# First loads in a new order, smaller and larger buffers, and another pacing of the inverse's tail

## The chip, the core and the metric

The kernel runs on one core of a Trainium2 chip. The time is device microseconds of one execution. A core has five engines that work in order, each with its own queue of instructions: TensorE (PE) multiplies, VectorE (DVE) and ScalarE (ACT) work element by element, GpSimd (POOL) does a few small operations here and casts while it transfers, SyncE (SP) only issues transfers. SP, ACT and POOL each issue DMA transfers from their own queue. SBUF holds the working tiles (128 partitions), PSUM the results of matmuls.

## What is computed

Four layers on x of 2048 x 576 in float32: two kinds, each used twice. A is a Fourier mixing of the normalized input; B is a gate by a long convolution that doesn't depend on x, so its value is the same in both uses.

```python
x = A_x
x = x + _A_ref(_layernorm(x), dft_seq_re, dft_seq_im, dft_hid_re, dft_hid_im)
x = x + _B_ref(_layernorm(x), B_k, B_v, B_shift_k, B_ssm_k, B_ssm_D)
x = x + _A_ref(_layernorm(x), ...)          # the same matrices
x = x + _B_ref(_layernorm(x), ...)          # the same k, v and kernels
...
# _A_ref:  y = Cr @ (x Wr^T) - Ci @ (x Wi^T)
# _B_ref:  kv = shift_conv(k, 4 taps) * v
#          y = causal_long_conv(kv, ssm_k) + kv * ssm_D ;  return q * y
```

## The kernel before

**Precision.** All matmuls are float32 to a reduced format (float32r). Each factor is split into a high part (ACT copies it, which rounds: line 84) and a low part (DVE subtracts: line 85), and a product is three matmuls: high by high, high by low, low by high. `split` is used for the C matrices, x, the weights and the convolution's data, so most rows of the profile bear these two lines.

**Layer A.** It takes U = C x first, then U W. `layer` walks four blocks of 512 columns (`tb`), two matrices (`g`, real and imaginary) and 16 row tiles (`k`): 128 steps n of 14 matmuls of 128 x 512 into PSUM tiles `s0` to `s3` and `rm`. For each step a C tile of 256 KB is loaded into a raw tile (`load_c`, ring `craw`, three tiles of NT = 512 words) and split into one of three tiles of the ring `cs`. The loads of step n + 2 are issued at step n, behind the previous C load (`load_after`: not before the last C load in the issue order, the `anchor`). A block's columns are multiplied by W later in `hidden`, in pieces of 27 matmuls of 128 x 288, which `finish` puts between the steps. `done0` stores the result xa.

**Branch B** is a generator, `branch`, whose steps are put between those of layer one. The long convolution is a transform of length 4096, factored in three parts. *F1* (steps n to 40): for 16 values of j and two sources (ssm_k and the gated k, v) a constant f1c is loaded (POOL, cast on the way), the source is built on DVE and split, twelve matmuls are made and four evacuations by ACT (line 395) fill two store buffers `so`, which ACT's queue stores to DRAM (`t`, line 396). Then W is loaded (`load_w`, raw ring `wl` of five) at steps 41 to 43. *Middle* (64 groups): load from `t` into a landing tile `land`, split to `df`, six matmuls with the constant `mc` (from midc), the spectra's product on DVE and ACT through `kk`, `p2` and `yf`, and, two groups later, three matmuls of the inverse, an evacuation by ACT into `vo` (line 449) and a store to `vd`. *Inverse, or i2* (32 pieces): the constant i2c is loaded by POOL into `fc`, a row of `vd` by SP into `land`, split, and six matmuls, evacuated into `vo` (line 460) and stored to `yb`. Twelve pieces run between the last middle groups, 20 behind them.

**Pacing.** Between step 44 (`W_END` + 1) and 111 (`I2_END`) the generator yields a number for each piece of its work, 3.1 for a middle group in all, 1.2 for an i2 piece, and is resumed until the sum spent has reached that share of the whole (`work`) which the steps' planned time has reached.

**Between the layers.** From step 113 (`PREP`) on, `get_x1` builds layer two's x: it loads xa, reads yb, gates (`gated`, DVE), stores xb, normalizes, stores y and splits the result into `mats`. Layer two does its first block in the same way and the other three by a Strassen scheme of seven products (`strassen`), which the change touches only by the C ring's size in the first 14 steps.

**Memory.** `flts` is one flat tile, whose words from `SC_AT` on hold the raw C tiles, and behind them, in turn, F1's buffers (`so`, `v`, `tmp`), the raw weights (`wl`), the middle's buffers (`res`, `kk`, `land`, `vo`, `p2`) and xa and yb. A tile laid over the words of an older one waits for its last use.

**The instruction order** on each engine's queue is fixed when the kernel is built, by a scheduler that follows the program's order and its own plan of times; it may put an instruction ahead of others of the same engine. In the built program of before, the start on PE is 24 f1 products, then the first step of layer one; SP's first issues are ssm_k, x, C, ssm_k, ssm_d, x, C.

Of the kernel before, what the change touches and what calls it, by code (L numbers as in the profile page):

```python
# [12 lines left out]
AF = mybir.ActivationFunctionType  # L13
# [9 lines left out]
NC = 4  # L23
REM = D - NC * P
EPS = 1e-5
PRE = 2
ASTAT = 8
XLEAD = 3
K_FIRST = 2
# [6 lines left out]
MID_LAG = 2  # L36
I2_FIRST = 37
I2_LATE = 4
PIECE = 3.6
STEP = 3.2  # L40
KP = 4
H = 2 * P
WIDE = 2 * NT
KR = 5
STAT = 20
STATIC = 14
B_LOAD = 15
# [10 lines left out]
def fnet_h3_kernel(ctx: ExitStack, tc: tile.TileContext, x, c_mat, w_re, w_im, k_pad, v, shift_k,  # L58
# [38 lines left out]
    def region_b(dt, name):  # L97
        return sb.tile([P, 6 * WIDE], dt, tag="rb", name=name)
# [11 lines left out]
    def lay(t, at, *sizes):  # L110

        for name, words, n in sizes:
            ring.setdefault(name, Ring()).tiles.extend(t[:, at + i * words:at + (i + 1) * words] for i in range(n))
            at += n * words
        assert at <= t.shape[1], (at, t.shape, sizes)
        return at

    def fresh(*names):
        for name in names:
            ring[name] = Ring()  # L120
# [24 lines left out]
            return nc.sync.dma_start(dst, src).ins  # L145

    def load_fr(dst, src):
        if pows:
            with tc.issue_after(pows[-1]):
                nc.gpsimd.dma_start(dst, src)  # L150
        else:
            nc.gpsimd.dma_start(dst, src)

    nc.vector.memset(mhalf, -0.5)
# [47 lines left out]
    W = []  # L202

    def load_w():
        lay(flts, SC_AT + 3 * NT, ("wl", D, 5))
        wg = region_a(FR, "w").rearrange("p (k n) -> p k n", k=9)
        for ch in range(9):
            w = two(wg[:, ch])
            raw = ring["wl"]()
            if ch < 8:  # L210
                nc.sync.dma_start(raw, (w_re if ch < 4 else w_im)[(ch % 4) * P:(ch % 4 + 1) * P, :])
            else:
                nc.sync.dma_start(raw[:REM], w_re[NC * P:, :])
                nc.sync.dma_start(raw[REM:], w_im[NC * P:, :])
            for lo, hi, sg in ((0, P, 1 if ch < 4 else -1),) if ch < 8 else ((0, REM, 1), (REM, P, -1)):
                if sg > 0:
                    split(w[lo:hi, 0, :], w[lo:hi, 1, :], raw[lo:hi])
                else:
                    nc.scalar.activation(w[lo:hi, 0, :], raw[lo:hi], AF.Copy, scale=-1.0)
                    nc.vector.scalar_tensor_tensor(w[lo:hi, 1, :], raw[lo:hi], -1.0,  # L220
                                                   w[lo:hi, 0, :].bitcast(F32), op0=OP.mult,
                                                   op1=OP.subtract)
            W.append(w)
            yield
        for ch in range(9):
            load_after(w_d[ch], wg[:, ch].bitcast(F32))
            yield
# [95 lines left out]
    def quads(v):  # L323
        return v.rearrange("p (a q) -> p a q", a=4)

    def branch():
        wt = []
        f1r = region_b(FR, "f1r")
        lay(f1r, 0, ("xf", 2 * D, 4), ("fc", 4 * P, 3))
        lay(flts, SC_AT + 3 * NT, ("so", D, 3), ("v", D, 2), ("tmp", D, 1))  # L330
        f1f = region_a(F32, "f1f")
        lay(f1f, 0, ("k", 2 * D, KR), ("wt", 2 * D, 2), ("land", D, 3), ("v", D, 1))

# [19 lines left out]
        def f1_loads(j, src):  # L353
            if j not in fcs:
                fcs[j] = quads(ring["fc"]())
                load_fr(fcs[j], f1c[j])
            r = ring["land" if src else "v"]()
            nc.sync.dma_start(r, (ssm_k if src else v)[:, j, :])
            if not src:
                if not wt:  # L360
                    load_w4()
                while loaded[0] < min((J + 4) // 2, 2 + j, j // 2 + KR):
                    load_k(loaded[0])
                    loaded[0] += 1
            return r, fcs[j]
# [42 lines left out]
        f1_products(*xf)  # L408
        yield
        m1 = region_b(FR, "mid")  # L410
        at = lay(m1, 0, ("df", 2 * D, 3), ("mc", 4 * P, 1))
        fresh("land", "fc")
        spare = at
        at = lay(m1, at, ("yf", D, 2))
        lay(m1, at, ("fc", 4 * P, 2))
        lay(flts, SC_AT + 3 * NT, ("res", D, 2), ("kk", D, 2), ("land", D, 2), ("vo", HD, 2), ("p2", HD, 1))
        mc = quads(ring["mc"]())
        raw = ring["kk"]()[:, :4 * P]
        nc.sync.dma_start(raw, midc.rearrange("p a q -> p (a q)"))
        nc.scalar.activation(mc, quads(raw), AF.Copy)  # L420
        lo, hi = slice(0, 64), slice(64, 128)

        def mid_forward(df):
# [72 lines left out]
        for i, (kind, hf, q) in enumerate(feeds):  # L496
            df, fc = halves.pop(i)
            if kind:
                i2_products(hf, q, fc, df)
            else:  # L500
                if len(yfs) == MID_LAG:
                    mid_inverse(*yfs.pop(0))
                    yield 0.4
                yfs.append((hf, q, mid_forward(df)))
            split_feed(i + 1)
            load_feed(i + 2)
            if i == last_mid:
                while yfs:
                    yield 0.4
                    mid_inverse(*yfs.pop(0))  # L510
                old = ring["fc"]
                held = [old.tiles[(old.n + m) % 2] for m in range(2)]
                fresh("fc")
                lay(m1, spare, ("fc", 4 * P, 2))
                ring["fc"].tiles.extend(held)
            yield 1.2 if kind else 2.7

    def gated(xa, j, late=False):
        mv, rs, _ = norm_stats(xa)
        q = ring["yb"]()  # L520
        (load_after if late else nc.sync.dma_start)(q, yb_d[j])
        nc.vector.scalar_tensor_tensor(q, xa, mv[:, 0:1], q, op0=OP.subtract, op1=OP.mult)
        nc.vector.scalar_tensor_tensor(q, q, rs, xa, op0=OP.mult, op1=OP.add)
        return q
# [15 lines left out]
    def load_x(j):  # L540
        if j < J:
            XL[j] = ring["x"]()
            nc.sync.dma_start(XL[j], x[:, j, :])
# [12 lines left out]
    def get_x1(j):  # L556
        if j in ready:
            return
        ready.add(j)
        xa = ring["xa"]()  # L560
        nc.sync.dma_start(xa, xa_d[j])
        xb = gated(xa, j)
        nc.sync.dma_start(xb_d[j], xb)
        y = normed_x(xb, xa, ring["xj"]())
        stored.append(nc.sync.dma_start(y_d[j // 2][:, j % 2, :], y).ins)
        X[j] = to_x(y, j)
# [2 lines left out]
        nc.sync.dma_start(out[:, j, :], gated(xa, j, True))  # L569

    pending = []
    lay(flts, SC_AT, ("craw", NT, 3))
    br = branch()
    wl = load_w()
    for used in range(1, K_FIRST + 1):
        next(br)
        load_x(used - 1)
        if used <= 2:
            load_c((0, 0, used - 1))
        if used == PRE:  # L580
            get_x0(0)
        if used == PRE + 1:
            get_x0(1)
    spent, total, paced = 0.0, 0.0, [0.0]

    def pieces(n):
# [4 lines left out]
    for n in range(W_END + 1, I2_END + 1):  # L591
        total += STEP + PIECE * pieces(n)
        paced.append(total)
    work = 64 * 3.1 + 32 * 1.2
    for n, whole in layer(get_x0, lambda j: x[:, j, :], done0, pending):
        if whole and n <= F1_END:
            want = K_FIRST + (F1_16 * n // 16 if n <= 16 else F1_16 + (32 - K_FIRST - F1_16) * (n - 16) // (F1_END - 16))
            while used < want:
                next(br)
                used += 1  # L600
            if n == F1_END:
                next(br)
        if whole and F1_END < n <= W_END:
            for _ in range(3):
                next(wl, 0)
        if n > W_END:
            if whole and pieces(n):
                finish(pending, 1)
            m = n - W_END - 1
            if m + 1 < len(paced):  # L610
                done_by = paced[m] + (paced[m + 1] - paced[m] if whole else STEP * 3 / 7)
            else:
                done_by = total
            while spent < work * done_by / total:
                spent += next(br, work)
        if not whole:
            continue
        if n >= W_SAVE and n % 2 == 0:
            next(wl, 0)
        m = n - PREP  # L620
        if m == 0:
            lay(flts, SC_AT + 3 * NT + 2 * D, ("xa", D, 2), ("yb", D, 2))
            lay(region_b(F32, "gate"), 0, ("xa", D, 4), ("yb", D, 4), ("xj", D, 2))
        if 0 <= m < TB * (TB - 1):
            get_x1(m)
# [318 lines left out]
```

## Time and profile before

| | us |
|---|---|
| median of the three runs shown (1243.41 to 1248.4) | 1248.28 |
| the profiled execution | 1246.32 |
| its span, first to last instruction | 1244.5 |

The stages in the profiled execution: F1 to about 208, the weights to 226, middle groups to about 600, the i2 tail to 652, building of layer two's x to about 706, layer two's first block to 845, the Strassen products to 1123, the last hidden products to the end.

A busy time is the time in which an engine executes; the idle time before an instruction is named with what ended it (`[1.67 <-ACT flts L395]`: PE sat idle for 1.67 us until ACT's instruction of line 395 was done). Tiles are named by the flat tile that holds them: `flts` is most buffers, `mid` and `f1r` the branch's matmul factors, `mats` x and the split C, `bk`, `s` and `rm` PSUM tiles, `early` the input x.

### The profile page before, as it was taken

Reading aid. Unit: us, or ns where it says so; the run is one execution under the profiler, and the core shown is the slowest. Engines: PE = TensorE matmul, PEld = TensorE weight load, DVE = VectorE, ACT = ScalarE, POOL = GpSimd, SP = SyncE. Lnnn points to the kernel's source line nnn. Section 1 sums busy time; section 2 is a strip of 40 time slices with the busy share of each in tenths; the row PEclk is TensorE's granted clock in tenths of the full one; section 3 lists DMA queues with packets and bytes.
Section 4 is the critical chain, followed back from the end, with each engine's and each line's share of the span. In section 5 each row is a group of like instructions: output and inputs, shape, how many; then the busy total and the mean of one; then the engine's idle time right before and its main releaser. Section 6 shows DMA issues by size and latency. Waiting matters only on the chain.

```text
span 1244.5 us, 18406 instructions
## 1 busy us (share of the span) xinstructions
PE 1192.8 (96%) x6320; PEld 1031.2 (83%) x6320; DVE 847.5 (68%) x1559; ACT 658.4 (53%) x1315; POOL 81.5 (7%) x116
## 2 busy tenths in 40 slices
PE   6999999899999999999789999999999999999997
PEld 5778888798888888888677798888878878879997
DVE  6999894668776676766338844666667668674674
ACT  6865565658766676765347823534344344460210
POOL 2210000000000000000213201000000000000111
PEclk9999999999999999999899999999999999999999
DMA  8989987646656665566788863765475478687631
GB/s 282 316 254 288 285 251 247 203 132 175 196 186 188 186 191 176 167 182 191 224 260 275 283 195 112 254 223 167 138 254 159 133 265 274 232 270 229 217 118 41
DMA packets 145968, 261.97 MB, mean 210 GB/s; under 512 B 15825, under 2 KB 44497, under 8 KB 145874
## 3 DMA queue, kind: packets, MB, share of 16 engines
q1 hardware_dynamic: 102674, 205.73, 52.6%
q10 hardware_dynamic: 36288, 42.48, 9.8%
q0 software_dynamic: 6912, 12.59, 3.9%
q8 instruction: 50, 0.82, 0.3%
q14 instruction: 44, 0.36, 0.1%
HBM read 194.09 MB, written 66.65 MB: 210 GB/s over the span
## 4 chain that ended last, share of the span: by engine, by line
PE 67%; DMA 14%; DVE 9%; ACT 6%; issue 3%; POOL 1%; SPq 0%; ACTq 0%; POOLq 0%; DVEq 0%
PE s L67 35%; PE bk L67 27%; PE rm L67 5%; DMA ph<-in_c_mat 2%; DMA flts<-in_c_mat 2%; DVE mats L85 1%; DMA flts<-vd 1%; DMA t<-flts 1%; ACT mats L84 1%; DMA vd<-flts 1%; DMA yb<-flts 1%; DVE ph L720 1%; DVE mid L85 1%; DMA gate<-xa 1%; ACT mid L84 1%
## 5 line engine op out<-in xcount | busy, mean ns | idle before, releaser
L67 PE MATMUL s<-mats 128*128 128x512 f32 x2094 | 527.1, 393 | 6.5 <-DVE mats L85 2.0
L67 PEld LDWEIGHTS s<-mats 128*128 128x128 f32 x2094 | 387.1, 189 | 84.6 <-DVE mats L85 6.0
L84 ACT ACTIVATE mats<-flts 128x512 fp32r<-128x512 f32 x209 | 130.6, 626 | 110.7 <-PE rm L67 66.7
L85 DVE TENSOR_TENSOR mats<-flts,mats 128x512 fp32r<-128x512 f32 x209 | 143.4, 688 | 59.3 <-ACT mats L84 56.2
L67 PE MATMUL bk<-mid 128*128 128x288 f32 x768 | 128.4, 303 | 16.8 <-ACT mid L84 4.9
L67 PEld LDWEIGHTS bk<-mid 128*128 128x128 f32 x768 | 113.5, 190 | 34.2 <-ACT mid L84 6.9
L85 DVE TENSOR_TENSOR mid<-flts,mid 128x576 fp32r<-128x576 f32 (+1 forms) x160 | 101.0, 637 | 53.2 <-ACT mid L84 50.2
L84 ACT ACTIVATE mid<-flts 128x576 fp32r<-128x576 f32 (+1 forms) x160 | 93.2, 586 | 64.8 <-DVE flts L438 38.2
L67 PE MATMUL bk<-w,u 128*128 128x288 f32 x864 | 119.7, 295 | 2.0 <-ACT flts L449 1.1
L67 PEld LDWEIGHTS bk<-w,u 128*128 128x128 f32 x864 | 117.4, 188 | 5.1 <-ACT flts L449 1.5
L67 PE MATMUL rm<-mats 128*128 128x512 f32 x338 | 104.8, 390 | 1.9 <-DVE flts L252 1.9
L67 PEld LDWEIGHTS rm<-mats 128*128 128x128 f32 x338 | 63.5, 188 | 15.4 <-issue 2.3
L67 PE MATMUL bk<-f1r 128*128 128x288 f32 x384 | 62.6, 307 | 11.8 <-DMA f1r<-in_f1c 6.0
L67 PEld LDWEIGHTS bk<-f1r 128*128 128x128 f32 x384 | 57.8, 196 | 17.8 <-ACT flts L395 7.0
L164 POOL TENSOR_TENSOR flts<-flts 128x1 f32<-128x1 f32 x40 | 35.4, 884 | 557.0 <-DVE flts L163 554.9
L67 PE MATMUL s<-t,mats 128*128 128x512 f32 x258 | 64.5, 389 | 0.0
L395 ACT ACTIVATE flts<-bk 128x288 f32<-128x288 f32 x128 | 48.1, 409 | 23.4 <-DMA t<-flts 12.6
L67 PEld LDWEIGHTS s<-t,mats 128*128 128x128 f32 x258 | 48.4, 188 | 10.1
L67 PE MATMUL bk<-mats 128*128 128x288 f32 (+1 forms) x340 | 56.7, 309 | 0.0
L435 DVE TENSOR_TENSOR flts<-bk,flts 128x288 f32<-128x288 f32 x64 | 29.2, 456 | 39.7 <-ACT flts L431 38.1
L67 PEld LDWEIGHTS bk<-mats 128*128 128x128 f32 x340 | 48.8, 188 | 2.0
L67 PE MATMUL s<-mats,u 128*128 128x512 f32 x198 | 50.0, 390 | 0.0
(148 smaller groups left out, 1530.0 us busy)
## 6 DMA issues: line engine op xcount, KB each, us to landing
flts<-in_c_mat SPq DMA_DIRECT2D x150, 256.0 KB, 3.5
ph<-in_c_mat SPq DMA_DIRECT2D x48, 512.0 KB, 4.1
t<-flts ACTq DMA_DIRECT2D x64, 288.0 KB, 4.1
flts<-t SPq DMA_DIRECT2D x64, 288.0 KB, 3.2
flts<-in_c_mat SPq DMA_DIRECT2D x36, 512.0 KB, 4.7
vd<-flts ACTq DMA_DIRECT2D x64, 144.0 KB, 3.2
flts<-vd SPq DMA_DIRECT2D x32, 288.0 KB, 3.5
mid<-in_i2c POOLq DMA_DIRECT2D x32, 256.0 KB, 4.9
```

The lines of the kernel that those rows point to most:

```text
L67: nc.tensor.matmul(ps, lhsT, rhs, start=first, stop=last, skip_group_check=more)
L84: nc.scalar.activation(h, src, AF.Copy)
L85: nc.vector.tensor_tensor(l, src, h.bitcast(F32), OP.subtract)
L164: pows.append(nc.gpsimd.tensor_tensor(rs, ve, mhalf, OP.pow).ins)
L395: nc.scalar.activation(so[:, c, :], ps[:, :HD], AF.Copy)
L435: nc.vector.tensor_tensor(p1, px[:, :HD], p1, OP.mult)
L720: nc.vector.tensor_tensor(src, src, r, OP.add)
```

## The change

- **First loads.** The loop that issued F1's first loads and x's first loads together is written out: x tile 0, then the branch's first step, C, x tile 1, C, normalization of x tile 0, the branch's second step. The first f1c is no longer cast by POOL but loaded by SP to a raw tile and copied by ACT; the later ones wait in POOL's order for the first power (`pows`). In the built program x tile 0 is SP's first issue, then f1c, ssm_k, C, x, C, x, ssm_k; on PE 12 f1 products stand ahead of the first step.
- **Two raw C tiles** instead of three (`CRAW`). The 512 words go to others: four `so` instead of three, seven `wl` instead of five, three `vo` instead of two.
- **midc** is loaded by POOL straight to `mc`, in place of an SP load into a `kk` tile and a copy by ACT.
- **The i2 tail.** After the last middle group `land` has four tiles: the two of `kk` are free and join. From there loads are issued four pieces ahead instead of two. An i2 piece counts 2.0 in the pacing instead of 1.2 (`I2_COST`).
- **Layer two's x:** the loads of xa and yb in `get_x1` go behind the last C load in the issue order.

```diff
+I2_COST = 2.0
+CRAW = 2
     def load_fr(dst, src):
-        if pows:
-            with tc.issue_after(pows[-1]):
-                nc.gpsimd.dma_start(dst, src)
-        else:
+        with tc.issue_after(pows[-1]):
             nc.gpsimd.dma_start(dst, src)
...
-        lay(flts, SC_AT + 3 * NT, ("wl", D, 5))
+        lay(flts, SC_AT + CRAW * NT, ("wl", D, 7))
...
-        lay(flts, SC_AT + 3 * NT, ("so", D, 3), ("v", D, 2), ("tmp", D, 1))
+        lay(flts, SC_AT + CRAW * NT, ("so", D, 4), ("v", D, 2), ("tmp", D, 1))
...
                 fcs[j] = quads(ring["fc"]())
-                load_fr(fcs[j], f1c[j])
+                if pows:
+                    load_fr(fcs[j], f1c[j])
+                else:
+                    raw = quads(ring["tmp"]()[:, :4 * P])
+                    nc.sync.dma_start(raw, f1c[j])
+                    nc.scalar.activation(fcs[j], raw, AF.Copy)
...
+        kk_at = SC_AT + CRAW * NT + 2 * D
...
-        lay(flts, SC_AT + 3 * NT, ("res", D, 2), ("kk", D, 2), ("land", D, 2), ("vo", HD, 2), ("p2", HD, 1))
+        at = lay(flts, SC_AT + CRAW * NT, ("res", D, 2))
+        lay(flts, at, ("kk", D, 2), ("land", D, 2), ("vo", HD, 3), ("p2", HD, 1))
         mc = quads(ring["mc"]())
-        raw = ring["kk"]()[:, :4 * P]
-        nc.sync.dma_start(raw, midc.rearrange("p a q -> p (a q)"))
-        nc.scalar.activation(mc, quads(raw), AF.Copy)
+        load_fr(mc, midc)
...
-            load_feed(i + 2)
+            load_feed(i + (4 if i > last_mid else 2))
             if i == last_mid:
                 while yfs:
                     yield 0.4
                     mid_inverse(*yfs.pop(0))
-                old = ring["fc"]
-                held = [old.tiles[(old.n + m) % 2] for m in range(2)]
-                fresh("fc")
-                lay(m1, spare, ("fc", 4 * P, 2))
-                ring["fc"].tiles.extend(held)
-            yield 1.2 if kind else 2.7
+                for name, t, at, words in (("fc", m1, spare, 4 * P), ("land", flts, kk_at, D)):
+                    old = ring[name]
+                    held = [old.tiles[(old.n + m) % 2] for m in range(2)]
+                    fresh(name)
+                    lay(t, at, (name, words, 2))
+                    ring[name].tiles.extend(held)
+                load_feed(i + 3)
+                load_feed(i + 4)
+            yield I2_COST if kind else 2.7
...
         xa = ring["xa"]()
-        nc.sync.dma_start(xa, xa_d[j])
-        xb = gated(xa, j)
+        load_after(xa, xa_d[j])
+        xb = gated(xa, j, True)
...
-    lay(flts, SC_AT, ("craw", NT, 3))
+    lay(flts, SC_AT, ("craw", NT, CRAW))
     br = branch()
     wl = load_w()
-    for used in range(1, K_FIRST + 1):
-        next(br)
-        load_x(used - 1)
-        if used <= 2:
-            load_c((0, 0, used - 1))
-        if used == PRE:
-            get_x0(0)
-        if used == PRE + 1:
-            get_x0(1)
+    load_x(0)
+    next(br)
+    load_c((0, 0, 0))
+    load_x(1)
+    load_c((0, 0, 1))
+    get_x0(0)
+    next(br)
+    used = K_FIRST
...
-    work = 64 * 3.1 + 32 * 1.2
+    work = 64 * 3.1 + 32 * I2_COST
```

More of the change, by code (lines that the diff above doesn't have):

```diff
@@ L25 @@
 EPS = 1e-5
-PRE = 2
 ASTAT = 8
@@ L621, in fnet_h3_kernel @@
         if m == 0:
-            lay(flts, SC_AT + 3 * NT + 2 * D, ("xa", D, 2), ("yb", D, 2))
+            lay(flts, SC_AT + CRAW * NT + 2 * D, ("xa", D, 2), ("yb", D, 2))
             lay(region_b(F32, "gate"), 0, ("xa", D, 4), ("yb", D, 4), ("xj", D, 2))
```

## The prediction

> **What bounds the kernel now.** I read the page first, then a table of stretches, then PE's waits, then the order of time around each wait that the diff touches.
>
> ```profile
> span 1244.5 us, 18406 instructions
> PE 1192.8 (96%) x6320; PEld 1031.2 (83%) x6320; DVE 847.5 (68%) x1559; ACT 658.4 (53%) x1315; POOL 81.5 (7%) x116
> ```
>
> PE is the bound: 51.7 us of its span is idle (1244.5 - 1192.8), and no other engine is near. The matmuls stay the same in number, so the change can win only idle time of PE and time at a lowered clock. The stretches show where that is (columns: PE, PEld, DVE, ACT, POOL busy, granted clock, DMA share, GB/s; the last two rows are from a second table of this view):
>
> ```profile
> 0.00:25.00 25.00, 15.65 (x56) 12.90 (x57) 15.94 (x52) 16.09 (x30) 5.17 (x12) 0.93 0.85 277
> 50.00:75.00 25.00, 24.09 (x111) 19.58 (x109) 24.05 (x50) 18.03 (x37) 6.30 (x7) 1.00 0.88 288
> 325.00:350.00 25.00, 23.06 (x114) 19.16 (x113) 18.50 (x34) 19.18 (x42) 0.00 (x0) 0.97 0.59 185
> 550.00:575.00 25.00, 25.00 (x149) 22.50 (x148) 15.68 (x31) 16.29 (x36) 1.06 (x2) 1.00 0.66 195
> 600.00:625.00 25.00, 18.87 (x95) 15.50 (x95) 6.82 (x12) 8.31 (x17) 3.77 (x7) 0.86 0.88 269
> 625.00:650.00 25.00, 20.90 (x131) 18.57 (x130) 8.94 (x14) 10.52 (x20) 3.69 (x7) 1.00 0.88 260
> ...
> 590.00:646.00 56.00, 44.85 (x251) 38.41 (x251) 19.95 (x36) 21.47 (x43) 10.71 (x20) 0.94 0.80 239
> 655.00:706.00 51.00, 48.02 (x204) 37.38 (x203) 44.51 (x127) 38.97 (x81) 16.64 (x20) 1.00 0.86 280
> ```
>
> The reader is to see two holes: the first 25 us (9.35 idle) and 590 to 646, the inverse's tail (11.15 idle, clock 0.94). In that tail DVE and ACT are idle for most of the time and the transfers are busy for 0.88: its limit is data that comes late.
>
> **The change part by part.**
>
> *First loads.* The order at the start:
>
> ```profile
> 1.18 0.42 SPq L543 DMA_DIRECT2D early<-in_x  x1
> 5.18 0.81 DVE L161 BATCH_NORM_STATS2 flts<-early 128x6 f32<-128x288 f32 x2
> 8.46 0.69 DVE L85 TENSOR_TENSOR mats<-flts,mats 128x512 fp32r<-128x512 f32 x1 [2.23 <-ACT mats L84]
> 9.07 0.15 DVE L163 TENSOR_SCALAR flts<-flts 128x1 f32<-128x1 f32 x1
> 9.31 0.99 POOL L164 TENSOR_TENSOR flts<-flts 128x1 f32<-128x1 f32 x1 [6.84 <-DVE flts L163]
> 9.80 0.80 DVE L161 BATCH_NORM_STATS2 flts<-early 128x6 f32<-128x288 f32 x2
> 10.64 3.29 PE L67 MATMUL bk<-f1r 128*128 128x288 f32 x12 [1.47 <-ACT f1r L84]
> 12.56 0.33 DVE L169 TENSOR_SCALAR flts<-flts 128x1 f32<-128x1 f32 x2
> 13.62 1.61 ACT L170 ACTIVATE early<-early,flts 128x576 f32<-128x576 f32 x2
> 15.14 1.25 ACT L175 ACTIVATE mats<-early 128x576 fp32r<-128x576 f32 x2
> 15.86 4.86 PE L67 MATMUL s<-mats 128*128 128x512 f32 x12 [1.93 <-ACT mats L175]
> ```
>
> The first block's products start at 15.86, when x tile 0 is normalized. Its statistics stood from 5.99, but DVE works in order: the add of L163 waited behind the C split (9.07), and the mean's row L169 behind two splits and x tile 1 (12.56). In the built order of the changed kernel x tile 0 is the first load (0.44 earlier), L163 stands ahead of the C split, L169 behind the statistics of x tile 1 alone, and one set of 12 f1 products instead of two stands ahead of the block. So: statistics from 4.7, L163 at 5.6, power done by 6.8, x tile 1's statistics (one load earlier than 9.80, some 8.5 to 9.3) then L169 at 9.3 to 10.1; normalizing 0.8, one evacuation 0.4, copy 0.65: products at 11.2 to 12. That is 4 us early, but the other 12 f1 products now come behind it (3.29 at the clock they had; half of that at the full one), and this step, 4.86 for 12 matmuls where 2.88 is usual (660.61, below), may meet the lowered clock again. Against it: f1c now crosses SP, then an ACT copy ahead of the first f1 product, and ssm_k moves from first to third load; both only shift f1, which no longer holds the block. I take 2.5 us, bounds 0 (DVE, 24.05 of 25 busy from 50 on, may give it back) and 4.5 (15.86 less 11.2).
>
> *Fourth store buffer of f1, midc over POOL.*
>
> ```profile
> 142.73 0.41 ACT L395 ACTIVATE flts<-bk 128x288 f32<-128x288 f32 x1 [2.18 <-DMA t<-flts]
> 143.19 0.67 PE L67 MATMUL bk<-f1r 128*128 128x288 f32 x3 [1.67 <-ACT flts L395]
> 222.68 0.33 SPq L419 DMA_DIRECT2D flts<-in_midc  x1
> 226.55 1.08 PE L67 MATMUL bk<-mid 128*128 128x288 f32 x6 [2.32 <-ACT mid L420]
> ```
>
> ACT waits at L395 for a store to free its buffer and PE for ACT: 1.67 us, which a fourth buffer covers (I take 1.7, because the wait is for the oldest of three stores, and of four it is older by another pair of evacuations; bounds 0 and 1.7). midc goes out at 222.68, behind the weights' splits whose words it takes, and PE idles 2.32. On POOL it is queued ahead of the first i2c loads with nothing of W ahead of it, and needs no ACT copy: 2.3 (0 if POOL's transfer came late; the gap then stays). The weights' two more tiles I put at nothing: they hide under layer blocks that need no W; without that cover they could give what this gap already counts.
>
> *Third buffer vo.*
>
> ```profile
> 346.02 0.59 ACT L251 ACTIVATE flts<-rm 64x512 f32<-64x512 f32 x1 [1.47 <-DMA vd<-flts]
> 347.48 0.70 PE L67 MATMUL rm<-mats 128*128 128x512 f32 x2 [1.94 <-DVE flts L252]
> 532.60 0.41 ACT L449 ACTIVATE flts<-bk 128x288 f32<-128x288 f32 x1 [1.78 <-DMA vd<-flts]
> 533.07 1.19 PE L67 MATMUL bk<-w,u 128*128 128x288 f32 x7 [1.12 <-ACT flts L449]
> ```
>
> Twice ACT stands at a vo whose store has not landed, and PE idles 1.94 and 1.12. The first also costs clock: 0.97 over 25 us is 0.75 us lost, and the dip runs on beyond that stretch; I put it at 1.5, twice the row. Together 4.6. As the middle transforms now come 11% denser (they are 64 x 3.1 = 198.4 of a paced work of 262.4, before of 236.8, so they pass through earlier in it), a third buffer may still be met at times: I take 3.5, bounds 0 and 4.6.
>
> By the Trainium skill, TensorE: Matmul & The Clock Gate, Part 1, the clock halves only after an idle window of about 3.4 us. Here it falls around a wait of 1.94 us, so the trace disagrees. By the page, removing such waits would win no clock, and the sum below would be some 3 us less, 1234.
>
> *Landing tiles and the tail.*
>
> ```profile
> 602.20 1.04 PE L67 MATMUL bk<-mid 128*128 128x288 f32 x6 [1.75 <-DMA mid<-in_i2c]
> 616.27 0.68 ACT L84 ACTIVATE mid<-flts 128x576 fp32r<-128x576 f32 x1 [2.97 <-DMA flts<-vd]
> 617.01 0.61 PE L67 MATMUL bk<-mid 128*128 128x288 f32 x1 [2.63 <-ACT mid L84]
> 633.24 1.96 PE L67 MATMUL bk<-mid 128*128 128x288 f32 x13 [1.20 <-ACT flts L460]
> ```
>
> These are its three kinds of wait: a constant, a landing tile, an output store. The diff's pacing, worked through step by step, ends the middle transforms at step 101 instead of 105 and puts the last 20 inverse pieces on steps 103 to 111, at most three each, instead of 105 to 111 with up to five; loads go out four pieces ahead instead of two. At stake: 11.15 idle, and 6.8 us at half clock (0.86) of which PE worked 4.3: 2.1 more, 13.2 in all. For it: the transfers at 550 to 575 are busy for 0.66 only, so there is room to load earlier. Against: 0.80 of 56 us is 45 us of transfer, and without the waits the stretch has 43; it fits only if some 9 us of it go out earlier, which is the room of one 25 us stretch at 0.66. I take 9, bounds 3 (one wait of the 2.63 kind and no more) and 13.2. The xa and yb reads of the next stage now go behind the last C load; the block that needs them is 15 steps away, so I put this at nothing (without that lead they would wait as long as a C load does).
>
> *Two raw C tiles.* The price of all this:
>
> ```profile
> SPq L145 <- DVE mats L85: 218.2, 128, 9.3
> DMA to landing us min/median/max: 2.7/3.4/7.2
> DMA to landing us min/median/max: 2.8/4.4/5.5
> 660.61 2.88 PE L67 MATMUL s<-mats 128*128 128x512 f32 x12
> 663.79 2.88 PE L67 MATMUL s<-mats 128*128 128x512 f32 x12
> 674.49 0.61 ACT L84 ACTIVATE mats<-flts 128x512 fp32r<-128x512 f32 x1
> 677.00 0.69 DVE L85 TENSOR_TENSOR mats<-flts,mats 128x512 fp32r<-128x512 f32 x1
> ```
>
> (Row 1: SP's own waits. Rows 2 and 3: landing of C loads in 24 to 75 and in 655 to 706.) A C load waits at SP's head until a split frees its tile; with two, it waits for the split of two steps before instead of three, and the x, k, v and store issues queued behind it wait too. Two steps must then hold one landing and one split: 2 x 3.18 = 6.35 us (660.61 to 663.79) against 3.4 + 2.5 early, which fits, and 4.4 + 2.6 at 655 (splits last 1.3, alone, to 3.2, as at 674.49 to 677.69), which is 0.65 too long, 0.33 a step. Over the 12 steps from the third of that stage this is 4 us; the three split tiles absorb some 1 us. I take 3 lost there (0 to 6), and 1 early (0 to 5, where a 7.2 us landing meets a busy DVE). From 225 to 590 steps with W products or middle transforms are longer: nothing.
>
> Sum: 2.5 + 1.7 + 2.3 + 3.5 + 9 - 4 = 15.0 us. The profiled execution took 1246.32 us (span 1244.5); it becomes 1231. That execution is 2.0 under the median of the runs shown, 1248.28.
>
> **The rivals.** *1. The tail stays bound by transfers.* For it, 0.88; against it, 0.66 before. The tail then gives 3: net 9, 1237 us. The Trainium skill, DMA: Bandwidth & Descriptors, Issuing engines are not separate DMA queues, is on its side: all loads share the same 16 engines, so deeper prefetch adds no rate. *2. The waits move on.* A store buffer more only lets ACT run into the next late thing, and DVE takes the start back: tail 3, midc 2.3, the rest 0, C -4: about 1245, which is no change. For it: the engines are in order, DVE is 24.05 of 25 busy from 50. Against: the tail's engines idle. *3. Slower: the C ring paces PE.* Its place is the first 16 steps, where no more than a few f1 products lie between, and the 16 from 655. It decides from an average landing of 3.85 us (6.35 less a split of 2.5). For it: 7.2 and 5.5 are seen, and what is queued behind a waiting C load at SP's head, k, v and the tail's loads, comes later too, so that of the gains only midc's 2.3, 3 of the tail and 3 of the buffers would be left, 8.3. At a landing of 4.4 in both places a step costs 0.28 too much, 9 us over 32 steps, and the sum turns; at 4.7 it is 0.43, 14 us, less 8.3: 5.5 slower, 1252; at 5.5 it would be 18 slower. I price it at 1252. Against it: the early median of 3.4.
>
> **How the numbers follow.** Forecast 0.50 (its own range 1222 to 1240), rival 1 0.20, rival 2 0.13, rival 3 0.17. 0.5% is 6 us, about what a measurement of this kernel can tell from no change. Faster: the forecast and rival 1 but for 0.02, and a little of rival 2: 0.70; same 0.14; slower, most of rival 3: 0.16. The range goes from 1220 (all gains at their upper bounds, 26.3, and no loss) to 1250, which leaves out most of rival 3.
>
> **What would show it.** First block product before 13; no L395 or L449 waiting for its store; the first middle product with no wait on midc; no stretch of 25 us between 575 and 650 with PE busy for under 23, and the clock at 1.00 there; C splits that wait for landing in at most a few steps at the start and in the stage before layer two. PE waiting on C splits for over 8 us in the two places together would make it wrong by rival 3, and a DMA share still near 0.88 with PE idle in the tail by rival 1.

## The result, and the profile after

The changed kernel took 1240.52 us (median of 19 runs, 1237.47 to 1243.53), the kernel before 1244.93 on the same chip: 0.9970 of it, 95% interval 0.9957 to 0.9983. Measured again beside the experiments it took 1241.22 against 1242.83, 0.9993 (0.9975 to 1.0010). By the medians it is 1.6 to 4.4 us faster, where 15 were forecast. Both are less than the 0.5% (6 us) that the prediction gave as about what can be told from no change, and the second interval includes no change. (The ratios are those on record; they can differ by up to 0.001 from the quotient of the two medians.) The profiled execution took 1238.42 us, its span is 1236.6.

The same table of stretches as in the prediction, of the changed kernel (PE, PEld, DVE, ACT, POOL busy, granted clock, DMA share, GB/s):

```profile
0.00:25.00 25.00, 17.63 (x70) 14.75 (x71) 18.25 (x59) 17.56 (x31) 5.22 (x13) 1.00 0.87 290
575.00:600.00 25.00, 24.14 (x148) 21.89 (x148) 10.31 (x15) 11.52 (x23) 4.20 (x8) 1.00 1.00 309
600.00:625.00 25.00, 25.00 (x153) 22.83 (x152) 9.16 (x14) 9.92 (x21) 4.24 (x8) 1.00 0.87 284
625.00:650.00 25.00, 25.00 (x131) 21.69 (x130) 16.97 (x40) 14.67 (x30) 3.87 (x5) 1.00 0.73 235
675.00:700.00 25.00, 22.53 (x110) 18.98 (x110) 20.76 (x56) 20.23 (x41) 7.72 (x9) 0.96 0.89 305
700.00:725.00 25.00, 25.00 (x141) 22.31 (x140) 5.68 (x10) 3.44 (x6) 0.00 (x0) 0.98 0.29 89
725.00:750.00 25.00, 25.00 (x156) 23.02 (x155) 7.08 (x15) 3.61 (x8) 1.08 (x2) 1.00 0.31 93
750.00:775.00 25.00, 20.68 (x86) 16.44 (x85) 16.03 (x43) 14.06 (x26) 5.12 (x7) 0.96 0.61 217
```

The tail is healed: from 600 to 650 PE is never idle and its clock is full. But a new hole stands at 750 to 775 (4.32 idle, clock 0.96), and the 50 us ahead of it look odd: DVE works for 5.68 and 7.08 of 25 us and the transfers for 0.3, and then DVE has 16.03 to do. Work that could have been done early was done late.

Of the other things that were to show: the first block product comes at 10.69, though its twelve products take 5.08 us, where 2.88 is usual. ACT at line 398 (395 of before) waits once for a store of `t`, 1.0 us, where in before it waits eleven times, 12.6 us in all, and at line 452 (449) it waits for no store. PE still waits for line 398 1.24 us at 47.23 and for line 452 0.96 at 268.67 and 0.86 at 576.31, so it was not a store that held these. The first middle product waits 3.35, not for midc but for `t`.

The steps show where the lead was won and lost. The table gives the time from the first product of one step on `s` to that of another, as the timeline lists them (a step has twelve products on `s` and two on `rm`; steps 128 to 159 are layer two's first block), in the profile of before and in two profiles of the changed kernel; the last column is what the prediction's terms say for that stretch.

| stretch | before | changed | changed, second profile | predicted |
|---|---|---|---|---|
| start to step 44 (f1) | 214.6 | -6.6 | -1.8 | -3.2 (2.5, 1.7, less 1) |
| 44 to 48 (first middle products) | 54.3 | +1.9 | +2.0 | -2.3 |
| 48 to 112 (middle and tail) | 385.4 | -14.3 | -14.3 | -12.5 (3.5, 9) |
| 112 to 136 | 111.4 | +1.7 | +3.9 | +3 |
| 136 to 148 | 38.1 | +6.5 | +6.8 | 0 |
| 148 to the first Strassen product | 38.1 | 0.0 | 0.0 | 0 |
| from there to the last product | 395.4 | +2.9 | +0.2 | 0 |

Each column is one execution: that of before took 1.4 us more than the median of its kernel, the two of the changed kernel 2.1 less and 1.9 more. The 2.9 of the last row stand in the first profile alone and are left aside.

The stretch from 136 to 148 loses what nothing in the sum stood for, and it does so in both profiles. Its wait, in the timeline of the changed kernel (3.85 us at 778.46 in the second profile):

```profile
771.45 0.73 PE L68 MATMUL s<-mats 128*128 128x512 f32 x2 [3.88 <-ACT mats L173]
772.63 4.14 PE L68 MATMUL s<-mats 128*128 128x512 f32 x10 [0.45 <-DVE mats L176]
```

PE waits for the copy and the split of an x tile, and the ten products behind it take 4.14 us where twelve take 2.88 at the full clock. SP's own rows in the same timeline say why the tile is late:

```profile
709.99 0.33 SPq L558 DMA_DIRECT2D xa<-flts  x1
...
721.95 0.33 SPq L558 DMA_DIRECT2D xa<-flts  x1
...
739.74 0.42 SPq L146 DMA_DIRECT2D flts<-xa  x1
740.21 0.42 SPq L146 DMA_DIRECT2D flts<-yb  x1
...
748.81 0.46 SPq L146 DMA_DIRECT2D flts<-xa  x1
...
757.36 0.45 SPq L146 DMA_DIRECT2D gate<-xa  x1
...
760.36 0.38 SPq L146 DMA_DIRECT2D gate<-xa  x1
```

and the same rows of before:

```profile
725.70 0.33 SPq L552 DMA_DIRECT2D xa<-flts  x1
...
728.19 0.33 SPq L561 DMA_DIRECT2D flts<-xa  x1
...
740.51 0.33 SPq L552 DMA_DIRECT2D xa<-flts  x1
...
742.60 0.32 SPq L561 DMA_DIRECT2D flts<-xa  x1
```

In before a tile's read goes out 2.5 us after its store. In the changed kernel tile 12 is stored at 709.99 and read at 739.74, 30 us later: `load_after` pins the read behind the C load that stands last when the program asks for tile 12, and it asks at step 137, not at 113. Tile 13 waits 27 us (721.95 to 748.81), and all four are gated and split on top of each other.

### The profile page after: what moved, and what is told of

It is laid out like the page before. It is cut to its first block, busy times and chain, and to the rows that moved or that the text cites. A ratio compares the mean times of both kernels' runs of the same rounds, so it can differ in the third digit from the quotient of the medians.

```text
span 1236.6 us, 18361 instructions
## 1 busy us (share of the span) xinstructions
PE 1192.3 (96%) x6320; PEld 1033.2 (84%) x6320; DVE 847.0 (68%) x1559; ACT 657.1 (53%) x1315; POOL 80.9 (7%) x116
## 4 chain that ended last, share of the span: by engine, by line
PE 70%; DVE 10%; DMA 10%; ACT 5%; issue 3%; POOL 1%; SPq 0%; ACTq 0%; POOLq 0%; DVEq 0%
PE s L68 36%; PE bk L68 28%; PE rm L68 6%; DMA ph<-in_c_mat 2%; DMA flts<-in_c_mat 2%; DVE mats L86 2%; ACT mats L85 1%; POOL flts L539 1%; DVE ph L725 1%; DMA gate<-xa 1%; DVE mats L176 1%; DMA xb<-gate 1%; DMA flts<-t 1%; POOL flts L162 1%; DVE f1f L383 1%
## 5 line engine op out<-in xcount | busy, mean ns | idle before, releaser
L68 PEld LDWEIGHTS bk<-mid 128*128 128x128 f32 x768 | 113.3, 188 | 25.1 <-ACT mid L85 8.2
L264 DVE TENSOR_TENSOR flts<-flts,bk 128x288 f32<-128x288 f32 x48 | 21.7, 452 | 69.0 <-PE bk L68 68.8
L398 ACT ACTIVATE flts<-bk 128x288 f32<-128x288 f32 x128 | 48.5, 410 | 14.7 <-PE bk L68 12.6
```

What stands on the lines that cost most here:

```text
L68: nc.tensor.matmul(ps, lhsT, rhs, start=first, stop=last, skip_group_check=more)
L264: nc.vector.tensor_tensor(r[:, cs], r[:, cs], ps[:, :HD], OP.add)
L398: nc.scalar.activation(so[:, c, :], ps[:, :HD], AF.Copy)
```

## The experiments

Each kernel is the changed one with the edit named, but for the third. The kernels of a set ran in turn on one chip with the kernel before, whose median there stands in brackets; each ran 6 to 12 times. The last three columns are from one profile each.

| set (before) | kernel | median | ratio to before (95%) | 48 to 112 | 112 to 136 | 136 to 148 |
|---|---|---|---|---|---|---|
| A (1244.04) | last four reads plain | 1237.11 | 0.9955 (0.9937 to 0.9972) | 371.0 | 113.6 | 43.6 |
| A | all reads plain | 1237.55 | 0.9956 (0.9939 to 0.9972) | 372.6 | 112.4 | 41.7 |
| A | before, with late reads | 1252.49 | 1.0071 (1.0048 to 1.0094) | 383.9 | 113.3 | 44.7 |
| A | old rings | 1241.68 | 0.9989 (0.9974 to 1.0004) | 378.9 | 112.4 | 43.9 |
| B (1242.83) | changed, second time | 1241.22 | 0.9993 (0.9975 to 1.0010) | 371.2 | 115.3 | 44.9 |
| B | last four plain, rm first | 1233.97 | 0.9936 (0.9913 to 0.9959) | 371.0 | 115.5 | 38.3 |
| B | inverse piece 1.2 | 1241.31 | 0.9990 (0.9973 to 1.0007) | 373.6 | 114.6 | 44.5 |
| B | two landing tiles | 1246.66 | 1.0025 (1.0005 to 1.0044) | 375.5 | 113.4 | 44.3 |
| C (1244.70) | five wl | 1240.33 | 0.9970 (0.9947 to 0.9993) | 370.8 | 114.3 | 45.0 |
| C | old start | 1239.58 | 0.9957 (0.9933 to 0.9981) | 372.9 | 114.7 | 45.0 |
| C | two vo | 1247.14 | 1.0029 (1.0006 to 1.0052) | 380.0 | 114.3 | 45.1 |
| C | third C tile early, five wl, last four plain, rm first | 1242.56 | 0.9985 (0.9961 to 1.0010) | 372.1 | 114.8 | 38.1 |
| D (1244.00) | three so | 1238.91 | 0.9960 (0.9942 to 0.9978) | 373.1 | 114.9 | 44.9 |
| D | midc by SP | 1240.50 | 0.9972 (0.9954 to 0.9990) | 371.1 | 113.4 | 44.6 |
| D | all plain, rm first | 1234.83 | 0.9930 (0.9902 to 0.9958) | 371.0 | 112.5 | 38.6 |
| D | old start, last four plain, rm first | 1234.49 | 0.9925 (0.9897 to 0.9952) | 372.6 | 115.7 | 41.8 |

The changed kernel itself came out at 0.9970 and 0.9993, so differences of under 0.3% between rows of different sets say nothing.

**The late reads.** One part taken back, for the last four tiles and for all, and the same part put alone into the kernel before.

```diff
-        load_after(xa, xa_d[j])
-        xb = gated(xa, j, True)
+        (load_after if j < TB * (TB - 1) else nc.sync.dma_start)(xa, xa_d[j])
+        xb = gated(xa, j, j < TB * (TB - 1))
```

> The changed kernel, but the reads of xa and yb for the last four tiles of layer two's x (12 to 15) go out where they stand in SP's order, as before the change; tiles 0 to 11 still wait for the last C load. Theory: the changed kernel is 19.0 us ahead at step 112 and loses 6.5 of it at steps 140 to 144, because xa of tile 12, stored at 709.99, is read only at 739.74. Then this kernel takes 5 to 6.5 us less than the changed one, 1234 to 1236 beside 1240.5, PE has no wait over 1 us in steps 136 to 144, and the lead over before at step 144 is 15 to 18 us in place of 10.8. Rival (DVE is simply overbooked there, or the two raw C tiles hold these steps back): within 1 us of the changed kernel, and the waits of 3.88 and 0.45 us stay.

> The changed kernel with all sixteen reads of xa and yb as before the change. Theory: the last four are all that matters, so it takes what the kernel with four plain reads takes, 1234 to 1236, within 1 us of it. Rival (the late reads were needed beside two raw C tiles, because a plain read that waits for its tile at SP's head holds up the C load behind it): 2 us or more slower than the kernel with four, with C splits that wait for their landing in steps 113 to 128.

> The kernel before, with this one part of the change: xa and yb of layer two's x go behind the last C load. Theory: it is 4 to 6.5 us slower than before, 1249 to 1251.5 beside 1245, with PE waiting for mats at steps 140 to 144 and nothing lost up to step 128. Rival (it hurts only together with two raw C tiles or the moved inverse pieces): within 1 us of before.

Before with late reads lost 8.5 us, more than expected, so this part costs by itself; 6.6 of it stand between 136 and 148. With all sixteen reads plain the time is that of four plain reads (1237.55 and 1237.11), so it is the last four that count, as expected. But both missed the 1234 to 1236 hoped for: with four plain reads step 144 is as far ahead as hoped (15.2 us), yet by step 148 the lead is 9.8. The timeline of that kernel (four plain reads):

```profile
775.39 0.61 PE L68 MATMUL rm<-mats 128*128 128x512 f32 x2
...
777.56 0.59 ACT L700 ACTIVATE flts<-rm 64x512 f32<-64x512 f32 x1
...
781.38 0.29 DVE L656 TENSOR_TENSOR flts<-flts 128x128 f32<-128x128 f32 x1 [2.62 <-DMA flts<-y]
781.59 0.69 DVE L670 TENSOR_TENSOR flts<-flts 128x512 f32<-128x512 f32 x1
...
782.19 0.67 DVE L701 TENSOR_TENSOR flts<-flts,rm 64x512 f32<-64x512 f32 x1
...
782.92 0.74 PE L68 MATMUL rm<-mats 128*128 128x512 f32 x2 [3.26 <-DVE flts L701]
```

The next step's `rm` needs the bank that line 701 empties. Line 701 could run from 778.2 on (777.56 + 0.59), but DVE works in order, and ahead of it stands line 656, which waits 2.62 us for a read of y. In before that line (696 there) stands behind such sums too and runs at 798.07, but PE makes its next `rm` products at 794.47 without a wait. So these can't go to the bank that line 696 still reads; which bank they have, and why the two programs differ in it, the record doesn't show.

**rm first.** The sums are made to follow line 701 in DVE's order; `rfree[0]` is the instruction of line 701.

```diff
-            next(builds[-1], None)
-            next(builds[-1], None)
+            with tc.issue_after(rfree[0]):
+                next(builds[-1], None)
+                next(builds[-1], None)
```

> The changed kernel as it is, beside the three that follow on the same chip. 0.997 of before, as measured first, and the wait of 3 to 4 us at steps 140 to 144 again; if the wait isn't there a second time, the loss between step 112 and the Strassen products was chance.

> The kernel with four plain reads, and DVE's sums for the Strassen factors (lines 656 to 670) put behind the evacuation of rm (line 701) that frees PE's bank. In the kernel with four plain reads PE stood 3.26 us at 782.92 until line 701 was done, because line 701 stood in DVE's order behind a sum that waited 2.62 us for a read of y, and the clock was halved for 3.4 us behind it: 5.5 us between steps 144 and 148. Theory: the late reads and this order are two waits in line, and only without both is the lead of step 112 kept; this kernel then takes 4 to 5.5 us less than the one with four plain reads, 1231.5 to 1233 beside 1237.1, with no PE wait over 1 us from step 136 to the first Strassen product. Rival (DVE has too much to do there): the wait moves on to the first Strassen products and the time stays within 1.5 us of 1237.

On the same chip 1241.22 became 1233.97, 7.2 us less, and 136 to 148 takes 38.3, as in before (38.1). The theory of two waits in line holds; the hoped 1231.5 to 1233 was missed by 1. (The new order with the reads still late was not run.) The stretch that had the hole, in the kernel with four plain reads and rm first:

```profile
750.00:775.00 25.00, 25.00 (x120) 21.12 (x119) 10.73 (x26) 10.90 (x20) 2.08 (x3) 1.00 0.55 179
```

PE is never idle, and DVE has 10.73 us of work where the changed kernel has 16.03. With all reads plain, or with the start of before, the time is the same within its interval; these three are the fastest of the kernels run. With the start of before 136 to 148 still takes 41.8 us, in its one profile: there PE waits 1.49 us at 784.42 for line 690, ACT's evacuation of U, and the granted clock is 0.50 from 785.78 to 789.20.

> All sixteen reads plain, and rm's evacuation first. Between step 112 and 136 the changed kernel's profiles lose 1.7 to 4.1 us against before; with plain reads alone or with the old rings alone 1.0. So this kernel should lose 1 there, nothing from 136 to the Strassen products, and take 1 to 3 us less than the kernel with four plain reads and rm first: 0.991 to 0.993 of before. If the loss at step 128 is only where the hidden products happen to lie, it is the same, 0.9936.

> The kernel with four plain reads and rm first, and with the start of before. The old start took nothing from the changed kernel (1239.6 beside 1240.3 to 1241.2); here it should again be within 1.5 us of the kernel with the new start, 0.9925 to 0.9950 of before. If the new start is worth 2.5 us after all, 0.9955 or more.

All plain reads win 3.0 us between 112 and 136 against four (112.5 and 115.5; in set A 112.4 and 113.6), as expected, but not in the median: that gain stays unproven.

**What healed the tail.** Three parts undone one by one.

```diff
-I2_COST = 2.0
+I2_COST = 1.2
...
-            load_feed(i + (4 if i > last_mid else 2))
+            load_feed(i + 2)
...
-        lay(flts, at, ("kk", D, 2), ("land", D, 2), ("vo", HD, 3), ("p2", HD, 1))
+        lay(flts, at, ("kk", D, 2), ("land", D, 2), ("vo", HD, 2), ("p2", HD, 1))
```

(With the second edit the two extra landing tiles go too.)

> The changed kernel with an inverse piece counted 1.2 in the pacing, as before; landing tiles and loads four ahead stay. If the 13 us of the tail come from the pacing (the transfers of the tail fit only when work goes out earlier), 6 to 10 us of the lead of 19 at step 112 are lost and waits for landing tiles are back between 600 and 650: about 1247. If the landing tiles and deeper loads bring them, it loses under 3: 1241 to 1243.

> The changed kernel with two landing tiles and loads two ahead in the tail; the pacing of 2.0 stays. If the pacing brings the tail's gain, it loses under 3 us: 1241 to 1243. If the landing tiles do, the waits for vd come back (three of 2.63, 1.41 and 0.85 before) with the halved clock: 6 to 9 us lost at step 112, about 1247.

> The changed kernel with two vo tiles. By the prediction a third one is worth 3.5 us between 345 and 535 (waits of 1.94 and 1.12 with the clock behind the first). By the trace it won nothing there, since at the same place PE now waits 1.64 us for the split of U; its worth is in the tail, where the kernel with the old rings shows waits for line 463 of 2.93 and 1.15 us. Then steps 48 to 104 stay within 1 us and 3 to 7 us are lost between step 104 and 112: 1243 to 1247.

Undoing the pacing costs nothing in the median, though waits are back in its profile (for i2c 2.27 us at 595.74 and 1.75 at 625.93, for a landing tile 2.21 at 605.24) and 48 to 112 takes 2.4 longer. So most of the tail's gain comes without the new pacing.

The landing tiles are worth 5.4 us (1246.66 less 1241.22), a little under the 6 to 9 expected, and the clock stays at 1.00 from 575 to 650. Without them PE waits for line 463 (460 of before), the inverse's evacuation into `vo`, but what ACT itself stood for is a row of `vd`, as expected. In the timeline of the kernel with two landing tiles:

```profile
605.91 0.68 ACT L85 ACTIVATE mid<-flts 128x576 fp32r<-128x576 f32 x1 [5.15 <-DMA flts<-vd]
606.50 0.61 ACT L85 ACTIVATE mats<-flts 128x512 fp32r<-128x512 f32 x1
...
607.02 0.39 ACT L463 ACTIVATE flts<-bk 128x288 f32<-128x288 f32 x1
...
607.47 1.07 PE L68 MATMUL bk<-mid 128*128 128x288 f32 x6 [2.32 <-ACT flts L463]
```

Line 463 stands behind the split of the landing tile in ACT's order, so the late row shows at PE as a wait for the evacuation.

The third `vo` is worth 6.8 (1247.14 against 1240.33 for the kernel with five wl in the same set), and 380.0 against 370.8 from 48 to 112. Here ACT stands at line 463 for a store of `yb` that has not landed. In the timeline of the kernel with two vo:

```profile
592.43 0.41 ACT L463 ACTIVATE flts<-bk 128x288 f32<-128x288 f32 x1 [2.16 <-DMA yb<-flts]
...
592.89 1.06 PE L68 MATMUL bk<-mid 128*128 128x288 f32 x6 [3.68 <-ACT flts L463]
...
611.25 0.41 ACT L463 ACTIVATE flts<-bk 128x288 f32<-128x288 f32 x1 [2.89 <-DMA yb<-flts]
...
611.71 1.06 PE L68 MATMUL bk<-mid 128*128 128x288 f32 x6 [1.62 <-ACT flts L463]
```

The third buffer works in the tail, at 593 and 612, and not at 346 and 532, where the prediction had put it: from 48 to 104 two vo cost 1.5 us against the changed kernel, from 104 to 112 7.4, a little outside the 1 and the 3 to 7 expected.

**Terms that did not come.** The start, the fourth so, midc and the W tiles undone one by one, and all rings together (three raw C tiles, three so, five wl, two vo).

> The changed kernel with the start of before: its order of first loads and f1c by POOL. The changed start puts step 0 at 10.7 to 11.5 us instead of 15.9, but at step 16 of the changed kernel's two profiles 1.1 us ahead and 1.8 us behind are left. If the start is worth what it shows at step 0, this kernel is 4 to 5 us slower: 1245. If DVE and the two raw C tiles take it back by step 16 anyway, it is within 1.5 us of the changed one, 1240 to 1242.

> The changed kernel with three so tiles, as before. The prediction put the fourth at 1.7 us (the wait of 1.67 at 143). In the kernel with the old rings these waits are back (0.68, 1.24, 0.55), while step 44 is within 1.2 us of the two profiles of the changed kernel's range. If the fourth is worth its 1.7, this kernel is 1 to 2.5 us slower; if two raw C tiles are what sets the first 44 steps, it is within 1 us.

> The changed kernel with midc loaded by SP to a kk tile and copied by ACT, as before. If the wait for t (3.0 to 3.8 us in every profile of the changed kernel) sets the first middle product, midc's path is hidden behind it: steps 48 and 112 and the time within 1 us of the changed kernel. If POOL's path is worth the predicted 2.3, step 48 comes 2 to 3 us later.

> The changed kernel with five raw tiles for W instead of seven. In the changed kernel PE stands 3.35 us at 216.03 until ACT has split the first row read from t: that read was issued at 211.38, right behind nine reads of W, although the last store of t was issued at 201.66. In before, with five tiles, the first read of t was issued at 211.01, ahead of five reads of W, 2.9 us behind the last store. Theory: seven W tiles let SP issue all of W first, and this is where midc's 2.3 us went; with five the wait is under 1 us and step 48 comes 2 to 5 us earlier against step 40 than in the changed kernel; 1237 to 1239 beside 1240.5. Rival (the wait is t's own way over DRAM): the wait stays over 2 us and the time is the same.

> The changed kernel with the rings of before: three raw C tiles, three so, five wl, two vo. The start, midc by POOL, the landing tiles, the pacing and the late reads stay. By the prediction's terms it gives back the 4 us of the C ring and loses 1.7 and 3.5: 1241.7. By the trace of the changed kernel, where the C ring cost 1.8 in the stage from 655 and the third vo won nothing: 1238.5 to 1241, with L395's wait for its store back (1 to 1.7 us) and the stage from step 113 to 128 shorter by about 2. If the C ring is what ate the gain: 1235 or less.

None of the first four is slower than the changed kernel: start, so and midc, each undone alone, are worth nothing that can be measured. That doesn't show that start and so together are worth nothing. In one profile each, the kernels with the old start or with three so begin step 44 at 210.2 and 210.8 us, inside the 208.0 to 212.7 of the changed kernel, while before does at 214.6 and before with late reads at 215.4. One may cover for the other; no run undoes just these two. For midc the trace shows why (the kernel with midc by SP):

```profile
213.34 0.34 SPq L424 DMA_DIRECT2D flts<-in_midc  x1
...
216.16 0.63 ACT L425 ACTIVATE mid<-flts 128x512 fp32r<-128x512 f32 x1 [0.45 <-DMA flts<-in_midc]
...
217.00 0.68 ACT L85 ACTIVATE mid<-flts 128x576 fp32r<-128x576 f32 x1 [0.22 <-DMA flts<-t]
...
217.74 0.85 PE L68 MATMUL bk<-mid 128*128 128x288 f32 x2 [3.08 <-ACT mid L85]
```

Even here the last thing to come is the first row of `t`, not midc. In the changed kernel midc goes out at 200.94, and PE waits 3.35 us at 216.03 for `t`. The theory that seven W tiles cause this fell: with five, the read of `t` stands ahead of W's last reads, and the wait is still 2.99 at 215.50. But that read still goes out at 211.13, 8.5 us behind the last store of `t` (202.62) and behind other reads of W in SP's order; whether this order causes the wait is open. The old rings reach step 16 at 71.5 us (before 75.2, changed 74.2 and 77.1), so two raw C tiles do cost f1 some 3 to 6 us there (the kernel with a third one early, below, is at 70.5); by step 44 it is at 209.0 (208.0 and 212.7), and without the third vo the tail loses more. Their sum is 1241.68, as the prediction's terms had it, from other shares.

**A version that did not work.** A third raw C tile until the middle begins, from words that are free then, with five wl, on top of the kernel with four plain reads and rm first.

> The kernel with four plain reads and rm's evacuation first (1234.0), with a third raw C tile until the middle transforms begin, and five raw W tiles. Theory: with two raw C tiles PE waits 2.4 to 2.8 us at 47 to 50 and 1.9 to 2.9 us at 74 to 77, with the old rings 0.81 and 0.50; so a third C tile early is worth 2 to 5 us at step 16, and the W tiles 2 to 4 us at step 48. Of that some goes into the waits between 270 and 580, so 3 to 5 us in all: 1229 to 1231. Rival (what is won early is lost where the middle transforms come denser): 1233 to 1235.

It took 1242.56, 0.9985 of before, where the kernel it adds to has 0.9936: the hope of 1229 to 1231 failed, and so did its rival. It is 4.7 us ahead of before at step 16, as hoped, and 1.6 behind at step 24. In its timeline:

```profile
90.54 0.68 ACT L85 ACTIVATE f1r<-f1f 128x576 fp32r<-128x576 f32 x1 [3.93 <-DMA f1f<-in_ssm_k]
...
92.66 0.67 PE L68 MATMUL bk<-f1r 128*128 128x288 f32 x3 [2.11 <-ACT flts L398]
...
108.74 0.68 ACT L85 ACTIVATE f1r<-f1f 128x576 fp32r<-128x576 f32 x1 [4.27 <-DMA f1f<-in_ssm_k]
...
110.29 1.09 PE L68 MATMUL bk<-f1r 128*128 128x288 f32 x3 [2.31 <-ACT flts L398]
```

f1's evacuations hold PE there, with four so. They are late because ACT, ahead of them in its order, stands for loads of ssm_k: 10.4 us in three waits between 75 and 118, where the kernel with four plain reads and rm first has none. Why these loads come late was not followed up.

## Why the prediction was wrong

*Landing tiles, pacing and vo.* Right in kind, a little small: 12.5 were forecast for step 48 to 112, 14.3 came. But the shares were wrong, so that the sum comes this near is partly luck. The prediction gave `vo` 3.5 for two waits at 346 and 532. The row of the first is line 251, which writes `rt` and no `vo`; in the changed kernel with two vo (1.62 us at 347.09) as with three (1.64 at 345.41) PE waits there for the split of U instead. 8.9 of the 14.3 are lost without the third `vo`, most of them in the tail, where the prediction had counted waits for line 460 among those that the landing tiles and the pacing would heal. The row of 633.24, which it read as an output store, is none: ACT had not stood idle at that line 460 (632.08). Rival 1 is out: DMA share 1.00, 0.87, 0.73 from 575 to 650, with 0.86 us of PE idle in the first of these stretches and none behind it.

*Reads of xa and yb.* This step failed: "the block that needs them is 15 steps away, so I put this at nothing (without that lead they would wait as long as a C load does)". It holds for tiles 0 to 11, which are asked for from step 113 on. Tiles 12 to 15 come from layer one's last hidden products and are asked for inside the block, at steps 137 to 140, three steps ahead of their use; a read that used to be hoisted to the moment of its store was pinned there. The prediction even named the condition in its bracket and did not check it for all sixteen. It cost 6.5 and 6.8 us, and undoing it with the wait behind it gave back 7.2.

*midc.* This step failed too: 2.3 us were forecast, and 44 to 48 became 1.9 and 2.0 longer. midc's wait was replaced by one for `t`: the first middle product stands one and a half steps earlier in PE's order (in the middle of step 45, in before behind step 46), and the read of `t` goes out only at 211.38, 9.7 us behind the last store of `t`, behind reads of W in SP's order. A wait was priced at its length, without asking what is late next.

*Start and so, with the C ring's early share.* The sum had 2.5 and 1.7 less 1, and start to step 44 became 6.6 and 1.8 shorter, so the stretch gave about what was forecast; which part gave it is not shown. The start's 4 us at step 0 did come (10.69, predicted 11.2 to 12), but by step 16 the lead is 1.1 us in one profile and -1.8 in the other, as rival 2 said. Two raw C tiles have a part in that, since they cost 3 to 6 us by step 16 and not 1; that DVE takes the rest is not shown.

*Two raw C tiles.* Forecast 3 lost in the stage before layer two, measured 1.7 and 3.9 from 112 to 136. With three raw tiles or with plain reads 1.0 is left, so both may have a part; single profiles that differ by 2.2 don't tell more. Of PE's two large waits there in the changed kernel, in its timeline, the larger is not for a C split but for U's:

```profile
669.21 3.99 PE L68 MATMUL s<-mats 128*128 128x512 f32 x11 [1.33 <-DVE mats L86]
...
697.22 3.29 PE L68 MATMUL s<-mats 128*128 128x512 f32 x8 [2.47 <-DVE u L86]
```

Rival 3 did not happen: of waits that can be for a C split this stage shows 1.33 and 0.27 us, far from 8.

The balance, by the table: of the 15.0 forecast, 4.2 to 4.3 are missing at the first middle products and 6.5 to 6.8 at the reads, while 48 to 112 gave 1.8 more. That leaves 5.7 to 6.1, where 1.6 to 4.4 were measured; the other stretches, -3.4 to 1.4 (f1), -1.3 to 0.9 (112 to 136) and 0.2 to 2.9 (the end), differ by as much between the two profiles, so the balance can't be drawn closer. Rival 2 came nearest, but its tail of 3 was wrong by more than 11.

## What to carry to other kernels

Where an order is pinned for a whole loop, check the last iterations by themselves: their data are made last and needed first, and a pin that is free for twelve tiles can hold four up. A wait that is removed is worth its length only if nothing else ends within that length; look for the second-latest input of the same instruction (here `t` beside midc, a bank of `rm` beside an x tile) before pricing it. Where PE waits for another engine, look at what that engine stood for: the same line 463 was late behind a read of `vd` in one kernel and behind a store of `yb` in another, and each has its own remedy. A part that costs nothing when it is undone alone may be covered by another part. An engine that is busy for 12.8 of 50 us and then has 16 of 25 to do shows work that was let out too late.

## What the hardware showed beside this

The clock falls to one half behind waits of quite different length. In stretches of 3.4 us of the changed kernel, each beginning within 1.5 us of where PE resumed:

```profile
74.20:77.60 3.40, 3.40 (x17) 2.88 (x18) 3.40 (x6) 2.88 (x7) 0.00 (x0) 1.00 0.78 247
216.50:219.90 3.40, 3.40 (x17) 3.40 (x16) 2.15 (x5) 2.84 (x7) 0.00 (x0) 0.51 0.72 220
670.50:673.90 3.40, 3.40 (x10) 2.62 (x9) 2.94 (x10) 2.69 (x7) 1.14 (x2) 0.50 0.99 339
772.90:776.30 3.40, 3.40 (x9) 2.67 (x9) 2.03 (x4) 1.46 (x3) 0.00 (x0) 0.50 0.66 205
```

The waits ahead of them are 2.44 us (74.18, no fall), 3.35 (216.03), 1.33 (669.21) and 3.88 with 0.45 (771.45). Each of the three falls fills such a stretch (0.50 to 0.51; 3.41 to 3.42 us by the trace's clock records), so it costs some 1.7 us, and a wait of 1.33 can bring one while one of 2.44 doesn't. The Trainium skill, TensorE: Matmul & The Clock Gate, Part 1, states a free-running window of 3413 ns; the length of the falls agrees with it. Its rule that an idle window of that length is what halves the clock doesn't fit the wait of 1.33.
